# Result rows on every 16th partition, stored by one transfer

## The chip, the core and the metric

The kernel runs on one core of one Trainium2 chip. The metric is the device time of one execution in microseconds; lower is better. The time of the kernel before is the median of three runs. One more execution was recorded by the hardware profiler, and every row below comes from that one.

A core has a matrix engine (TensorE, PE in the profile), three engines for elementwise work (VectorE or DVE, ScalarE or ACT, GpSimd or POOL), and SyncE (SP), which here only issues transfers. Each engine runs its own list of instructions in order. Transfers between the main memory (HBM) and the on-chip memory (SBUF, 128 partitions) are issued by an engine and carried out by 16 DMA engines. TensorE writes to PSUM, an accumulator memory of 128 partitions.

## What is computed

One decoding step for two batches: attention over a cache of 4096 positions with 32 heads of 128, an output projection, a small feed-forward network, and a sigmoid gate that mixes the two. Cut to what matters:

```python
# x: (2, 1, 512); k_cache, v_cache: (2, 32, 4096, 128); wq: (512, 4096); wo: (4096, 512)
g = sigmoid((x * gate_w).sum(-1, keepdims=True))
q = (x @ wq) as (2, 32, 1, 128)
p = softmax(q @ k_cache^T * 128 ** -0.5)
a = (p @ v_cache) as (2, 1, 4096) @ wo
b = relu(x @ w1) @ w2                  # w1: (512, 1376), w2: (1376, 512)
out = g * a + (1 - g) * b              # (2, 1, 512), bfloat16
```

The K and V caches are 64 MB each; with the weights, 145.43 MB are read. The output is two rows of 512 numbers, 2 KB.

## The kernel before

The program is a list of operations for each engine, written out in one order by Python; a name given as `signal` marks an operation, and `waits` names the marks that another operation needs. An engine signals by counting up one semaphore, so a wait is for a count: whoever waits for a late operation of an engine also waits for all earlier ones of it.

**Loading.** SyncE issues almost all transfers, in one queue: wq, then 16 units of K and 16 of V, 4 MB each, into three buffers `kv` (L262 to L267). A unit is issued when the unit three places earlier has been used up: K units by four transposes on VectorE (`k_turn`, L380), V units by 32 matmuls (`v_unit`, L442). Behind the third unit stands w1, which waits for the q projection (`pe_q`, L267). Behind all units come the last 96 rows of w2 in eleven small pieces (L269, of 14 rows down to 2), wo in two halves (L270, L271), and the other rows of w2 in three pieces, w2b, w2c, w2d (L273).

**Start.** GpSimd clears and builds constants (L214 to L241); the last is `ptm`, 4096 elements per partition, marked `c_ptm`. ScalarE loads x and the gate's weights. VectorE copies the transposed x into `xTw` (L288), multiplies it for the gate (L289), and TensorE projects q (L320). The q values are spread into `qbuf` (L345), and the scores of the first K unit can start (L396).

**Middle.** Each K unit is transposed on VectorE and multiplied on TensorE; after four units a softmax is taken (L406 to L422), GpSimd spreads the probabilities into `ptm` (L425), and V units are multiplied with them. At the ninth transposed piece the first layer of the feed-forward network runs (`ffn_h`), and VectorE writes its result, scaled by one minus the gate, into `hT` (`ffn_relu`, L367 and L370). `hT` is [128, 11, 2]: eleven chunks of the hidden layer, the two batches side by side.

**End.** `o_gather` collects the attention output of a batch and writes it into `oW`, [128, 32, 2], a column for each batch (L483). Then `project` and `ffn_f` add up the result in one PSUM region of 128 partitions and 128 columns. They use `fin_row`: for each chunk r four matmuls, one for each block c of 128 output columns, with the two columns of `oW` or `hT` as weights. Block c goes to column group c of TensorE, so it lands on partitions 32c and 32c+1: batch b of block c is on partition 32c + b. That is 32 x 4 matmuls with wo and 11 x 4 with w2. `store` copies the region into `out_sb` (L507). SyncE then stores batch 0 and ScalarE batch 1, each as four rows of 128 numbers (`out_row`, L274 to L277), both behind that copy, and SyncE waits until both have arrived (L278).

Of the kernel before, what the change touches and what calls it, by code (L numbers as in the profile page):

```python
# [3 lines left out]
dt = mybir.dt  # L4
# [82 lines left out]
def bass_gated_mix__gqa_block_cached__dense_activation_relu__decode_kernel(  # L87
# [18 lines left out]
    sb = nc.alloc_sbuf_tensor  # L106
# [14 lines left out]
    wreg = sb("wreg", [128, 16384], dt.bfloat16)  # L121
    w2 = sb("w2", [128, 11, 512], dt.bfloat16)
# [18 lines left out]
    s4 = sb("s4", [32, 4, 128], dt.bfloat16)  # L141
    X2 = sb("X2", [128, 2, 8, 128], dt.float32)
    O_sb = sb("O_sb", [32, 2, 128], dt.bfloat16)
    oW = sb("oW", [128, 32, 2], dt.bfloat16)
    hT = sb("hT", [128, 11, 2], dt.bfloat16)
    out_sb = sb("out_sb", [128, 128], dt.bfloat16)

    PSF = nc.alloc_psum_tensor("PS", [128, 4096], dt.float32)
# [4 lines left out]
    def psf(p0, p1, c0, n):  # L153
        return PSF[p0:p1, c0:c0 + n]
# [8 lines left out]
    H_C0 = MISC + 72  # L163
    L_C0 = MISC + 96
    O_C0 = MISC + 128
    R_C0 = MISC + 256
    FIN_C0 = 0
# [4 lines left out]
    sem = {n: nc.alloc_semaphore("sem_" + n) for n in names}  # L172
# [4 lines left out]
    def marker(name):  # L177
        m = mk.get(name)
        if m is None:
            m = _Marker()  # L180
            mk[name] = m
        return m
# [14 lines left out]
    def freed(what):  # L197
        kind, u = what
        return marker(f"kt_{4 * u + 3}") if kind == "k" else marker(f"pe_v_{u}")


    def pool(fn, waits=(), signal=None):
        P.add("pool", fn, waits=[marker(w) for w in waits], signal=marker(signal) if signal else None)

    def dve(fn, waits=(), signal=None, dwaits=()):
        P.add("dve", fn, waits=[marker(w) for w in waits], signal=marker(signal) if signal else None, dwaits=dwaits)

    def act(fn, waits=(), signal=None, dwaits=()):
        P.add("act", fn, waits=[marker(w) for w in waits], signal=marker(signal) if signal else None, dwaits=dwaits)

    def pe(fn, waits=(), signal=None, dwaits=()):
        P.add("pe", fn, waits=[marker(w) for w in waits], signal=marker(signal) if signal else None, dwaits=dwaits)
# [5 lines left out]
         waits=["c_i16z"], signal="c_i16")  # L218
# [5 lines left out]
                                   in_=mask3[:].rearrange("p (t f) h c -> p t f h c", t=4)[:, :, 0],  # L224
                                   pattern=[[-32, 4], [-4, 4], [-1, 4]],
                                   compare_op=ALU.not_equal, fill=1.0, base=0, channel_multiplier=1),
         waits=["c_m3z"], signal="c_m3")
# [4 lines left out]
         waits=["c_s1"], signal="c_s2")  # L232
    pool(lambda g: g.affine_select(out=sell[:, 16:32], in_=sell[:, 16:32], pattern=[[8, 4], [32, 4]],
                                   compare_op=ALU.is_ge, fill=0.0, base=7, channel_multiplier=-1),
         waits=["c_s2"], signal="c_sell")
# [3 lines left out]
         waits=["c_s4z"], signal="c_s4")  # L239
    pool(lambda g: g.memset(selx[:], 0.0), signal="c_selx")  # L240
    pool(lambda g: g.memset(ptm[:], 0.0), signal="c_ptm")  # L241


    wq_in = A_wq.rearrange("(p t) n -> p (t n)", t=4)
# [11 lines left out]
    def sp(fn, waits=(), dwaits=()):  # L256
        P.add("sp", fn, waits=waits, dwaits=dwaits)
# [4 lines left out]
    for n, what in enumerate(order):  # L262
        waits = [freed(order[n - NSLOT])] if n >= NSLOT else []
        sp(lambda e, what=what: e.dma_start(kv[:, slot_of(what), :], unit_in(what)).then_inc(sem_slot[slot_of(what)], 16),  # L264
           waits=waits)
# [5 lines left out]
    sp(lambda e: e.dma_start(wreg[:, 8192:16384], wo_in[:, 8192:16384]).then_inc(sem["wo1"], 16))  # L271
    for name, r0, r1 in (("w2b", 0, 4), ("w2c", 4, 8), ("w2d", 8, 10)):
        sp(lambda e, name=name, r0=r0, r1=r1: e.dma_start(w2[:, r0:r1, :], w2a_in[:, r0:r1, :]).then_inc(sem[name], 16))  # L273
    def out_row(e, b):  # L274
        return e.dma_start(out[b:b + 1].rearrange("b s (c n) -> (b s c) n", n=128), out_sb[b::32, :]).then_inc(sem["out"], 16)

    sp(lambda e: out_row(e, 0), waits=[marker("dve_out")])  # L277
    sp(lambda e: e.wait_ge(sem["out"], 32))  # L278


    def gate():
# [82 lines left out]

    def ffn_relu():
        for b in range(2):
            dve(lambda v, b=b: v.tensor_scalar(out=hT[:, 0:10, b], in0=PSF[:, H_C0 + b:H_C0 + 20:2], scalar1=0.0,  # L367
                                               scalar2=gm[:, b:b + 1], op0=ALU.max, op1=ALU.mult),
                waits=["pe_h", "dve_gm"])
            dve(lambda v, b=b: v.tensor_scalar(out=hT[0:96, 10, b:b + 1], in0=psf(0, 96, H_C0 + 20 + b, 1), scalar1=0.0,  # L370
                                               scalar2=gm[0:96, b:b + 1], op0=ALU.max, op1=ALU.mult),
                waits=["pe_h", "dve_gm"], signal=f"dve_h{b}")

# [47 lines left out]
    def sm_spread(g):  # L421
        dve(lambda v: v.transpose(out=ET_sb[:, :], in_=E_sb[:, :]),  # L422
            waits=[f"act_exp{g}"] + ([f"pool_pt{g - 1}_3"] if g else []), signal=f"dve_et{g}")
        for hq in range(4):
            pool(lambda e, g=g, hq=hq: e.tensor_copy(  # L425
                out=ptm[32 * hq:32 * hq + 32, g % 2, :, :, :, hq, :],
                in_=ET_sb[32 * hq:32 * hq + 32, :].rearrange("p (r u a c) -> p r u a c", r=16, u=4, a=2)),
                waits=[f"dve_et{g}", "c_ptm"] + ([f"pe_v_{4 * g - 5}"] if g >= 2 else []), signal=f"pool_pt{g}_{hq}")


    def v_unit(v):
# [38 lines left out]
    def o_gather(b):  # L470
        for u in range(8):
            pe(lambda e, u=u, b=b: e.matmul(psf(0, 32, O_C0, 128), lhsT=selx[:, 28 - 4 * u:60 - 4 * u], rhs=X2[:, b, u, :],  # L472
                                            start=(u == 0), stop=(u == 7)),
               waits=[f"dve_x{8 * b + u}_3"] + ([f"dve_rinv{b}", "dve_selx"] if u == 0 else []),
               signal=(f"pe_O{b}" if u == 7 else None))
        dve(lambda v, b=b: v.tensor_scalar(out=O_sb[:, b, :], in0=psf(0, 32, O_C0, 128), scalar1=rinv[:, b:b + 1],
                                           scalar2=gb[0:32, b:b + 1], op0=ALU.mult, op1=ALU.mult),
            waits=[f"pe_O{b}", f"dve_rinv{b}", "dve_g"], signal=f"dve_O{b}")
        for dq in range(4):
            pe(lambda e, dq=dq, b=b: e.matmul(psf(0, 128, R_C0 + 32 * b, 32), lhsT=s4[:, dq, :], rhs=O_sb[:, b, 32 * dq:32 * dq + 32],  # L480
                                              start=(dq == 0), stop=(dq == 3), tile_position=(0, 0)),
               waits=([f"dve_O{b}", "c_s4"] if dq == 0 else []), signal=(f"pe_R{b}" if dq == 3 else None))
        dve(lambda v, b=b: v.tensor_copy(out=oW[:, :, b], in_=psf(0, 128, R_C0 + 32 * b, 32)), waits=[f"pe_R{b}"], signal=f"dve_oW{b}")  # L483


    def fin_row(r, first, last, lhsT, rhs, dw, waits, signal):
        for c in range(4):
            pe(lambda e, c=c: e.matmul(psf(32 * c, 32 * c + 2, FIN_C0, 128), lhsT=lhsT, rhs=rhs[:, c * 128:(c + 1) * 128],  # L488
                                       start=first, stop=last, tile_position=(0, 32 * c), skip_group_check=True),
               dwaits=(dw if c == 0 else []), waits=(waits if c == 0 else []), signal=(signal if c == 3 else None))  # L490

    def project():
        dve(lambda v: v.memset(psf(0, 128, FIN_C0, 128), 0.0), waits=["act_exp2"], signal="dve_fin0")
        for r in range(32):
            dw = {0: [(sem["wo0"], 16)], 16: [(sem["wo1"], 16)]}.get(r, [])
            fin_row(r, r == 0, False, oW[:, r, :], wreg[:, r * 512:(r + 1) * 512], dw,
                    ["dve_oW0", "dve_oW1", "act_exp3", "dve_fin0"] if r == 0 else [], None)

    def ffn_f():
        for n, r in enumerate([10, *range(10)]):  # L500
            m = 96 if r == 10 else 128
            dw = {10: [(sem["w2a"], 16 * len(W2A))], 0: [(sem["w2b"], 16)], 4: [(sem["w2c"], 16)], 8: [(sem["w2d"], 16)]}.get(r, [])
            fin_row(r, False, r == 9, hT[0:m, r, :], w2[0:m, r, :], dw, ["dve_h0", "dve_h1"] if n == 0 else [],
                    "pe_fin" if r == 9 else None)

    def store():
        dve(lambda v: v.tensor_copy(out=out_sb[:, :], in_=psf(0, 128, FIN_C0, 128)), waits=["pe_fin"], signal="dve_out")  # L507
        act(lambda e: out_row(e, 1), waits=["dve_out"])


    gate()
# [7 lines left out]
    for i in range(64):  # L519
        k_turn(i)  # L520
        if i >= 1:
            k_scores(i - 1)
        flush()
        if i == 8:
            ffn_h()
            late.append(ffn_relu)
        if i % 16 == 0 and i:
            g = i // 16 - 1
            sm_max(g)
            sm_exp(g)  # L530
            late.append(lambda g=g: sm_spread(g))
        if i == 40:
            o_denominator(0)
        if i >= 19 and i % 4 == 3:
            v = i // 4 - 4
            if i == 63:
                k_scores(63)
                sm_max(3)
                sm_exp(3)
                sm_spread(3)  # L540
            v_unit(v)
            late.append(lambda v=v: v_extract(v))
        if i == 52:
            late.append(lambda: o_gather(0))
# [41 lines left out]
```

## Time and profile before

| | |
|---|---|
| median of three runs | 347.62 us (347.56 to 348.02) |
| the profiled execution | 347.98 us |
| its span, first to last instruction | 346.5 us |
| busy in the span | PE 203.3 us, weight loads 76.7, DVE 182.4, ACT 13.9, POOL 20.9 |
| mean granted TensorE clock | 0.80 of full speed |
| read from HBM | 145.43 MB, 420 GB/s over the span |
| DMA queues, packets | q1 (SyncE's) 5816, q10 (ScalarE's) 14, instruction queues 12 |

Views used below: the page's slices (the span in 40 equal parts, each digit a busy share in tenths); the chain of waits, which follows the work that ended last back from the end, at each step to what released it; the timeline, which lists instructions in order of time (start, length, engine, line, operation, output<-inputs, shape, count, and in brackets the idle time before it and what ended it); waits by engine; and the DMA view of a short window, cut into 40 slices. "SPq" and "ACTq" are the queues from which SyncE and ScalarE issue transfers; the length of such a row is that of the issue, not of the transfer.

### The profile page before, as it was taken

To read this page: it belongs to the slowest core of one execution; us is meant where nothing else is said; L and a number is where in the kernel's file an instruction comes from. 1 tells how busy PE (TensorE), PEld (TensorE's weight loads), DVE (VectorE), ACT (ScalarE), POOL (GpSimd) and SP (SyncE) were. 2 spreads that over 40 slices of the span, in tenths; PEclk is the share of its full clock that TensorE was granted. 3 is DMA by queue.
4 is the path that set the end of the run, shared out by engine and by line. 5 is a ranking of instruction groups with operands and counts; after the bars stand their busy time and mean duration, and the time that the engine had idled before them with its cause. 6 is when DMAs were issued, how large, how long until landed. Compare 5 with 4: busy or idle time off the path is not lost.

```text
span 346.5 us, 3037 instructions
## 1 busy us (share of the span) xinstructions
PE 203.3 (59%) x1334; PEld 76.7 (22%) x1334; DVE 182.4 (53%) x177; ACT 13.9 (4%) x48; POOL 20.9 (6%) x36
## 2 busy tenths in 40 slices
PE   0419959773755729175855839074785839422283
PEld 0203333221211203021221313021421213110052
DVE  0848877990917356391918355391648367211120
ACT  1030000000000000000000000000000000000000
POOL 8400000020000000020000000020000000200000
PEclk9967978999685958789695969789696969666576
DMA  8999999999999999999999999999999999999993
GB/s 322 446 431 431 404 453 443 427 429 424 424 426 436 443 431 431 429 424 431 435 429 439 431 435 424 422 431 435 439 426 443 427 424 431 423 435 435 395 412 154
DMA packets 5842, 145.61 MB, mean 420 GB/s; under 512 B 739, under 2 KB 838, under 8 KB 1222
## 3 DMA queue, kind: packets, MB, share of 16 engines
q1 hardware_dynamic: 5816, 145.43, 98.1%
q8 instruction: 10, 0.16, 0.2%
q14 instruction: 2, 0.02, 0.0%
q10 hardware_dynamic: 14, 0.00, 0.0%
HBM read 145.43 MB, written 0.00 MB: 420 GB/s over the span
## 4 chain that ended last, share of the span: by engine, by line
DMA 70%; DVE 14%; PE 12%; SPq 2%; issue 1%; DVEq 0%
DMA kv<-in_A_k_cache_dram 53%; DVE kt L380 11%; DMA w<-in_B_w_dram 10%; PE PS L396 8%; DMA kv<-in_A_v_cache_dram 8%; PE PS L442 4%; SPq L269 1%; DVE X L456 1%; DVE mpad L406 1%; DVE ET L422 1%; PE PS L488 0%; SPq L264 0%; DVE X L453 0%; DVE mrow L408 0%; DVE mmax L409 0%
## 5 line engine op out<-in xcount | busy, mean ns | idle before, releaser
L396 PE MATMUL PS<-kt,qbuf 128*128 128x512 bf16 x512 | 149.8, 446 | 93.9 <-DVE kt L380 93.7
L380 DVE STREAM_TRANSPOSE kt<-kv 128x2048 f32<-128x2048 f32 x64 | 144.0, 2285 | 102.8 <-DMA kv<-in_A_k_cache_dram 102.2
L396 PEld LDWEIGHTS PS<-kt,qbuf 128*128 128x128 bf16 x512 | 50.5, 108 | 190.3 <-DVE kt L380 117.8
L442 PE MATMUL PS<-kv,ptm 128*16 128x512 bf16 x512 | 37.2, 442 | 23.0 <-DMA kv<-in_A_v_cache_dram 23.0
L425 POOL COPY ptm<-ET 32x512 bf16<-32x512 bf16 x16 | 9.7, 607 | 276.5 <-DVE ET L422 275.8
L442 PEld LDWEIGHTS PS<-kv,ptm 128*16 128x16 bf16 x512 | 12.8, 98 | 45.8 <-issue 35.7
L453 DVE TENSOR_SCALAR X<-PS,maskc 128x128 f32<-128x128 f32 x16 | 5.1, 319 | 30.9 <-PE PS L442 30.9
L456 DVE SCALAR_TENSOR_TENSOR X<-PS,maskc,X 128x128 f32<-128x128 f32 x48 | 16.8, 351 | 1.7
L351 ACT ACTIVATE qbuf<-PS 32x4 bf16<-32x4 bf16 x32 | 5.7, 178 | 110.7 <-PE PS L396 110.1
L417 ACT ACTIVATE E<-PS,negm 128x512 bf16<-128x512 f32 x4 | 2.7, 687 | 154.5 <-DVE negm L413 154.5
L472 PE MATMUL PS<-X,selx 128*32 128x128 f32 x32 | 5.3, 336 | 0.0
L283 PE MATMUL PS<-ident,x_sb 3*128 3x3 bf16 x4 | 0.3, 168 | 8.1 <-DMA x_sb<-in_gate_w_dram 8.1
L361 PE MATMUL PS<-xT,wreg 128*128 128x2 bf16 (+1 forms) x44 | 2.8, 200 | 3.6 <-DMA wreg<-in_B_w_dram 3.6
L472 PEld LDWEIGHTS PS<-X,selx 128*32 128x32 f32 x32 | 4.4, 142 | 1.9 <-issue 1.4
L286 DVE COPY xT<-PS 128x12 bf16<-128x12 bf16 x1 | 0.2, 169 | 8.4 <-PE PS L283 8.4
L488 PE MATMUL PS<-wreg,oW 128*2 128x128 bf16 x128 | 2.6, 242 | 3.4 <-DMA wreg<-in_A_wo_dram 3.0
L220 POOL MEMSET qbuf<- 128x5120 bf16 x1 | 4.4, 4370 | 0.0
L507 DVE CAST out_sb<-PS 128x128 bf16<-128x128 f32 x1 | 0.3, 291 | 7.6 <-PE PS L488 7.6
L288 DVE COPY xTw<-xT 128x8 bf16<-128x8 bf16 x1 | 3.9, 3862 | 0.0
L406 DVE TENSOR_REDUCE mpad<-PS 128x1 f32<-128x512 f32 x4 | 2.7, 676 | 2.1 <-PE PS L396 2.1
L361 PEld LDWEIGHTS PS<-xT,wreg 128*128 128x128 bf16 (+1 forms) x44 | 2.7, 161 | 4.1 <-DMA wreg<-in_B_w_dram 4.1
L289 DVE TENSOR_TENSOR xg<-xT 128x8 f32<-128x8 bf16 x1 | 3.6, 3629 | 0.0
(58 smaller groups left out, 40.5 us busy)
## 6 DMA issues: line engine op xcount, KB each, us to landing
kv<-in_A_k_cache_dram SPq DMA_DIRECT2D x16, 4096.0 KB, 26.2
kv<-in_A_v_cache_dram SPq DMA_DIRECT2D x16, 4096.0 KB, 18.7
wreg<-in_A_wq_dram SPq DMA_DIRECT2D x1, 4096.0 KB, 12.4
wreg<-in_A_wo_dram SPq DMA_DIRECT2D x2, 2048.0 KB, 29.9
wreg<-in_B_w_dram SPq DMA_DIRECT2D x1, 1376.0 KB, 27.3
w<-in_B_w_dram SPq DMA_DIRECT2D x2, 512.0 KB, 33.4
w<-in_B_w_dram SPq DMA_DIRECT2D x1, 256.0 KB, 33.9
x_sb<-in_A_x_dram ACTq DMA_DIRECT2D x1, 2.0 KB
```

Source lines behind the costliest of these rows:

```text
L220: pool(lambda g: g.memset(qbuf[:], 0.0), signal="c_qbuf")
L288: dve(lambda v: v.tensor_copy(out=xTw[:, :, 0:2], in_=xT), waits=["dve_xT", "c_xTw"], signal="dve_xTw")
L351: act(lambda a, out=out, src=src: a.activation(out=out, in_=src, func=ACT.Copy), waits=[f"pe_sc_{4 * uh + 3}"], signal=f"q_1_{uh}_{hq}")
L361: return e.matmul(psf(0, m, H_C0 + 2 * ft, 2), lhsT=cols, rhs=xT3[:, t, 0:2], start=(t == 0), stop=(t == 3))
L380: dve(lambda v: v.transpose(out=dst, in_=pairs[:, :, 32 * k:32 * k + 32, :]), waits=([f"pe_sc_{i - NKT}"] if i >= NKT else []), dwaits=([s ...
L396: pe(lambda e, j=j, pos=pos, c=c, cc=cc: e.matmul(psf(0, 128, (g % 2) * BANK, 512), lhsT=qbuf[:, u % 8, j, 32 - pos:160 - pos], rhs=kt16[: ...
L406: dve(lambda v, g=g: v.tensor_reduce(out=mpad[:, 0:1], in_=psf(0, 128, (g % 2) * BANK, 512), axis=AX.X, op=ALU.max), waits=[f"pe_sc_{16 * ...
L425: pool(lambda e, g=g, hq=hq: e.tensor_copy(out=ptm[32 * hq:32 * hq + 32, g % 2, :, :, :, hq, :], in_=ET_sb[32 * hq:32 * hq + 32, :].rearra ...
L442: pe(lambda e, n=n, t=t, a=a, r16=r16, grp=grp, u4=u4, rows=rows: e.matmul(psf(32 * t, 32 * t + 16, V_B * BANK, 512), lhsT=ptm[:, grp % 2, ...
L453: dve(lambda e, src=src, dst=dst: e.tensor_scalar(out=dst, in0=src, scalar1=maskc[:, 0:1], scalar2=None, op0=ALU.mult), waits=[f"pe_v_{v}" ...
L456: dve(lambda e, src=src, dst=dst, c=c: e.scalar_tensor_tensor(out=dst, in0=src, scalar=maskc[:, c:c + 1], in1=dst, op0=ALU.mult, op1=ALU.add),
L472: pe(lambda e, u=u, b=b: e.matmul(psf(0, 32, O_C0, 128), lhsT=selx[:, 28 - 4 * u:60 - 4 * u], rhs=X2[:, b, u, :], start=(u == 0), stop=(u ...
```

## The change

The two columns of weights move apart. `oW` and `hT` get 32 columns for each chunk instead of 2; batch 0 stands in column 0 and batch 1 in column 16. GpSimd clears both tensors once, behind `ptm`. The matmuls of `fin_row` take 17 columns as weights (0 to 16), so block c of batch b lands on partition 32c + 16b, and the 15 columns between give zeros. The result rows are then every 16th partition of `out_sb`, eight rows, and one transfer from SyncE stores them. ScalarE's transfer and `out_row` are gone; SyncE waits for one transfer. Operations that write `hT` and `oW` wait for the memsets, and the copies into `ptm` name the mark of the last memset, `c_oW`, in place of `c_ptm`. The order of all other instructions stays.

```diff
-    oW = sb("oW", [128, 32, 2], dt.bfloat16)
-    hT = sb("hT", [128, 11, 2], dt.bfloat16)
+    oW = sb("oW", [128, 32, 32], dt.bfloat16)
+    hT = sb("hT", [128, 11, 32], dt.bfloat16)
...
     pool(lambda g: g.memset(ptm[:], 0.0), signal="c_ptm")
+    pool(lambda g: g.memset(hT[:], 0.0), signal="c_hT")
+    pool(lambda g: g.memset(oW[:], 0.0), signal="c_oW")
...
-    def out_row(e, b):
-        return e.dma_start(out[b:b + 1].rearrange("b s (c n) -> (b s c) n", n=128), out_sb[b::32, :]).then_inc(sem["out"], 16)
-
-    sp(lambda e: out_row(e, 0), waits=[marker("dve_out")])
-    sp(lambda e: e.wait_ge(sem["out"], 32))
+    sp(lambda e: e.dma_start(out.rearrange("b s (c n) -> c (b s) n", n=128),
+                             out_sb[0::16, :]).then_inc(sem["out"], 16),
+       waits=[marker("dve_out")])
+    sp(lambda e: e.wait_ge(sem["out"], 16))
...
-            dve(lambda v, b=b: v.tensor_scalar(out=hT[:, 0:10, b], in0=PSF[:, H_C0 + b:H_C0 + 20:2], scalar1=0.0,
+            dve(lambda v, b=b: v.tensor_scalar(out=hT[:, 0:10, 16 * b], in0=PSF[:, H_C0 + b:H_C0 + 20:2], scalar1=0.0,
                                                scalar2=gm[:, b:b + 1], op0=ALU.max, op1=ALU.mult),
-                waits=["pe_h", "dve_gm"])
-            dve(lambda v, b=b: v.tensor_scalar(out=hT[0:96, 10, b:b + 1], in0=psf(0, 96, H_C0 + 20 + b, 1), scalar1=0.0,
+                waits=["pe_h", "dve_gm", "c_hT"])
+            dve(lambda v, b=b: v.tensor_scalar(out=hT[0:96, 10, 16 * b:16 * b + 1], in0=psf(0, 96, H_C0 + 20 + b, 1), scalar1=0.0,
...
-                waits=[f"dve_et{g}", "c_ptm"] + ([f"pe_v_{4 * g - 5}"] if g >= 2 else []), signal=f"pool_pt{g}_{hq}")
+                waits=[f"dve_et{g}", "c_oW"] + ([f"pe_v_{4 * g - 5}"] if g >= 2 else []), signal=f"pool_pt{g}_{hq}")
...
-        dve(lambda v, b=b: v.tensor_copy(out=oW[:, :, b], in_=psf(0, 128, R_C0 + 32 * b, 32)), waits=[f"pe_R{b}"], signal=f"dve_oW{b}")
+        dve(lambda v, b=b: v.tensor_copy(out=oW[:, :, 16 * b], in_=psf(0, 128, R_C0 + 32 * b, 32)), waits=[f"pe_R{b}", "c_oW"], signal=f"dve_oW{b}")
...
-            pe(lambda e, c=c: e.matmul(psf(32 * c, 32 * c + 2, FIN_C0, 128), lhsT=lhsT, rhs=rhs[:, c * 128:(c + 1) * 128],
+            pe(lambda e, c=c: e.matmul(psf(32 * c, 32 * c + 17, FIN_C0, 128), lhsT=lhsT, rhs=rhs[:, c * 128:(c + 1) * 128],
...
-            fin_row(r, r == 0, False, oW[:, r, :], wreg[:, r * 512:(r + 1) * 512], dw,
+            fin_row(r, r == 0, False, oW[:, r, 0:17], wreg[:, r * 512:(r + 1) * 512], dw,
...
-            fin_row(r, False, r == 9, hT[0:m, r, :], w2[0:m, r, :], dw, ["dve_h0", "dve_h1"] if n == 0 else [],
+            fin_row(r, False, r == 9, hT[0:m, r, 0:17], w2[0:m, r, :], dw, ["dve_h0", "dve_h1"] if n == 0 else [],
...
         dve(lambda v: v.tensor_copy(out=out_sb[:, :], in_=psf(0, 128, FIN_C0, 128)), waits=["pe_fin"], signal="dve_out")
-        act(lambda e: out_row(e, 1), waits=["dve_out"])
```

## The prediction

> **What bounds the kernel now.** I read the page's first line and its slices first, then the chain of waits in order of time, then the last microseconds instruction by instruction, and last the movement of the DMA engines in those microseconds.
>
> ```profile
> span 346.5 us, 3037 instructions
> ...
> DMA  8999999999999999999999999999999999999993
> ```
>
> The digits are the busy share of the 16 DMA engines in 40 slices: 9 from the second slice to the last but one. 145.43 MB must be read, and the kernel is the time that these reads take, plus a head and a tail. The change touches neither the reads nor their order, so only two places can matter: whatever could let the DMA queue run dry, and the tail after the last byte has come in. The tail in the chain of waits (start, length, what was waited for):
>
> ```profile
> 309.26 33.75 DMA w<-in_B_w_dram
> 343.01 0.04 issue
> 343.05 0.60 PE PS L488 x12
> 343.65 0.04 issue
> 343.69 0.41 PE PS L488 x8
> 344.10 0.02 issue
> 344.13 0.29 DVE out_sb L507
> ```
>
> The last weights (w2) end a wait at 343.05 and another at 343.69; after that come eight matmuls, one copy out of PSUM, and the two stores. The timeline of the stores (start, length, engine) and the wait list of SyncE's queue (total, times, longest):
>
> ```profile
> 344.44 0.60 SPq L275 DMA_DIRECT2D out_dram<-out_sb  x1
> 344.45 0.61 ACTq L275 DMA_DIRECT2D out_dram<-out_sb  x1
> ```
>
> ```profile
> SPq L278 <- DMA out_dram<-out_sb: 1.4, 1, 1.4
> ```
>
> So 0.41 + 0.29 + 0.60 + 1.4 = 2.7 us, with the gaps 2.8 us (343.69 to 346.5), is all that the output side of the change can work on. What the DMA engines did in it, from 345.5 to 346.3 in 40 slices of 0.02 us:
>
> ```profile
> GB/s 0 0 0 0 0 0 0 0 13 26 0 13 0 0 0 0 0 0 0 0 0 0 0 0 0 0 13 26 0 13 0 0 0 0 0 0 0 0 0 0
> ```
>
> Two equal bursts: slices 8 to 11 (345.66 to 345.74) and 26 to 29 (346.02 to 346.10). The view of each half says that the first is queue q1 (SyncE) and the second q10 (ScalarE), eight packets each. So although both issues run side by side, the second row leaves 18 slices, 0.36 us, after the first, and the kernel waits for it.
>
> **The change, part by part.**
>
> *ScalarE's store goes (gain).* The second burst falls away: -0.36 us. Nothing is queued behind it on ScalarE, whose last other work ended at 295.2 us.
>
> *SyncE's store carries eight rows instead of four.* Issues of like size with nothing beside them are the small w2 pieces of L269; the chain shows that of 8 rows and that of 4 rows (the seventh and the tenth piece):
>
> ```profile
> 306.27 0.29 SPq L269
> 307.28 0.29 SPq L269
> ```
>
> Eight rows cost no more to issue than four. Four rows made eight packets inside 0.08 us; queue q10 carried 14 packets in the whole run, which is rows plus one end packet for each row for x (2+2), the gate (1+1) and the output (4+4), so each row had an engine of its own. With two rows on each of four engines there are 12 packets. A row's packet starts and ends within about a slice, so I add +0.02 us; bounds 0 and +0.08 (a second burst's full length).
>
> *The issue itself.* It took 0.60 us beside the other and 0.29 us for a lone piece. If the first burst was held back by the sharing, it now starts up to 0.31 us sooner; if the issues were served one after the other, SyncE's first, it starts when it did. The bursts stand 0.36 us apart, close to one lone issue after the other and far from being interleaved, so I take 0; ends 0 and -0.31 us. The Trainium skill, "DMA: Bandwidth & Descriptors", section Issuing engines are not separate DMA queues, says that issuing from several engines saves only the sequencers' time for issuing, and since that is usually small, by this rule dropping the second queue would gain nothing and the sum would be about +0.06 us; the bursts say otherwise here.
>
> *Weights of 17 columns.* All 172 loads of L488 change from 2 to 17 columns. The nearest rows are the 16-column loads of the V products, also four column groups and at the same granted clock of 0.50:
>
> ```profile
> 319.25 0.14 PEld L442 LDWEIGHTS PS<-kv,ptm 128*16 128x16 bf16 x8 [7.01 <-issue]
> 343.69 0.10 PEld L488 LDWEIGHTS PS<-w,hT 128*2 128x2 bf16 x8 [0.33 <-DMA w<-in_B_w_dram]
> ```
>
> Eight loads take 0.14 instead of 0.10 us: +0.04 us on the path, for the last eight matmuls. The 128 projection loads and the first 20 of the feed-forward end before 343.05 with PE idle for 0.46 us; 5 ns each on the 84 after 340.5 is 0.42 us, just covered. Of the 16 at 343.05, PE has 0.04 us to spare before 343.69; were none of their loads hidden, they add 0.08. Bounds 0 and +0.12 us. 17 rows of output cost nothing more: 32 matmuls of 512 columns into 16 rows take 3.59 us, 0.45 for four, 0.11 for each 128 columns, and the 16 of 128 columns into 2 rows at 343.05 take 0.60 us, 0.15 for four: fewer rows are no faster. The skill's "TensorE: Matmul & The Clock Gate", section LDWEIGHTS (loading the stationary operand), gives a load as columns divided by 1.2 ns, an estimate of 12.5 ns more for each, 0.10 us for eight, which would make the whole sum -0.24 us.
>
> *Strided copies.* L483 writes oW every 64 bytes instead of every 4; it takes 0.20 us at 336.09, and the projection it feeds waits for weights until 340.56, 3 us later. L367 and L370 at 50.12 cost four times 0.2 us, with 32 elements at most: nothing. Without those waits a slower L483 would be paid in full.
>
> *Two more memsets on GpSimd.* 352 and 1024 elements behind ptm's 4096 at 3.50 us (0.85 ns each): 0.3 + 0.9 = 1.2 us, ending near 13.7 instead of 12.46. The new waits on them stand before L367 (50.12), L483 and the first L425 (73.40): over 36 us late, none stops anything queued behind. But they hold something else:
>
> ```profile
> 8.63 3.86 DVE L288 COPY xTw<-xT 128x8 bf16<-128x8 bf16 x1
> 8.86 3.63 DVE L289 TENSOR_TENSOR xg<-xT 128x8 f32<-128x8 bf16 x1
> 8.96 3.50 POOL L241 MEMSET ptm<- 128x4096 bf16 x1
> ...
> 19.93 1.27 ACT L345 ACTIVATE qbuf<-PS 32x32 bf16<-32x32 bf16 x4 [0.49 <-PE PS L339]
> ```
>
> ```profile
> 25.32 11.76 PE L396 MATMUL PS<-kt,qbuf 128*128 128x512 bf16 x40 [5.43 <-DVE kt L380]
> ```
>
> A copy and a product of eight elements took 3.6 to 3.9 us and ended at 12.49, with ptm's memset. They will now probably end near 13.7, and q with them: 21.20 + 1.2 = 22.4 us. The first scores start at 25.32 behind the first K transpose, so 4.1 us of cover eats 1.2. The w1 load, issued behind q at 19.92, moves to 21.1, in a queue that has K units to bring until 44.0, when VectorE's wait for the third one ends. Cost 0; gone the cover, 1.2 us.
>
> Sum: -0.36 + 0.02 + 0 + 0.04 + 0 = **-0.30 us**. The profiled execution took 347.98 us (span 346.5 and 1.5 around it) and would take 347.7; it lies 0.36 above the median, so I put the sum on the median: 347.62 - 0.30 = **347.3 us**.
>
> **The rivals.**
>
> A, the lone issue also sends sooner. For: 0.29 against 0.60 us, and x's first packets at the head came 0.9 us after its issue began, SyncE's row 1.2 us after. Against: x's issue was shared too. Sum -0.36 - 0.31 + 0.06 = -0.61: 347.0 us.
>
> B, nothing is gained: the later burst was only the slower write, and eight rows in one transfer take as long as two of four (+0.36 given back). For: eight rows must leave either way. Against: a burst is 0.08 us long, so the 0.36 is not the writing. 347.62 + 0.06 = 347.7 us.
>
> C, slower: GpSimd's longer memset run. The DVE copies wait for its end, q is late, the scores are late, K slots come free late and the DMA queue runs dry once. Price 1.2 us, less the output's 0.3: 348.5 us; laid bare, with nothing saved at the end, 348.8. It decides only when q slips by more than 4.1 us and then by more than the 12 us for which K units are still queued when the fourth K unit is issued (31.87 to 44.0). Nothing in the profile brings 1.2 near that.
>
> That the store does not change as said is excluded for the issue: a single output transfer remains. Whether its eight rows spread over four engines is open; on one engine, eight rows and an end at about 0.02 us make 0.2 us, which lies between the likeliest case and B.
>
> **How the numbers follow.** Likeliest case 0.43, A 0.28, B 0.18, C 0.10, anything larger on the gaining side 0.01. Less than 0.2%, about 0.7 us, is what a measurement of this kernel can tell from no change: 346.92 and 348.32 are the edges. The likeliest and B lie inside. A stands 0.1 us from the edge, and the three runs before already differ by 0.46 us, so about half of A counts as faster, 0.14, and with the larger gains and the likeliest's lower tail 0.18. Slower is C, 0.10. The same: 0.72. The likeliest's own range is its bounds -0.67 to -0.16 (0 to +0.08 and 0 to +0.12 at their upper ends): 346.95 to 347.5. With A's scatter below and B's above (348.02 was seen before) I widen to **346.8 to 348.0**; C is left out.
>
> **What would show it.** One burst at the end with q1 alone in it, 12 packets, and q10 at 6 packets in all; the span's end 2.5 us (A: 2.2) behind the start of the last eight matmuls instead of 2.8. SyncE's output issue near 0.29 us: A is right if its burst also starts under 1.0 us after the issue. Eight 17-column loads in about 0.14 us. The copy into xTw and the product behind it ending near 13.7 us while the first scores stay at 25.3 and the last w2 wait at 343.7. The forecast is wrong if the first scores move, if a slice of the DMA row falls, or if the one transfer takes over 2 us from issue to the end as the two did.

## The result and the profile after

| | before | changed |
|---|---|---|
| median | 347.72 us (347.51 to 348.06, 20 runs) | 347.19 us (346.84 to 347.82, 20 runs) |
| the profiled execution | 347.98 us, span 346.5 | 347.82 us, span 346.6 |

The ratio is 0.9985, with a 95% interval of 0.9978 to 0.9992: 0.15% faster, 0.53 us between the medians. That is less than the 0.2% that the prediction gave as the least that can be told from no change, but the interval leaves out 1. The forecast was 347.3 us, in a range of 346.8 to 348.0; the change itself was forecast as -0.30 us.

The profiled execution of the changed kernel is the slowest of its 20: its last weights came in 0.38 us later than in that of before. So the tails can be compared, but not the two spans. The page of the changed kernel, queue lines (packets, MB, share):

```profile
q1 hardware_dynamic: 5820, 145.43, 98.1%
q8 instruction: 10, 0.16, 0.2%
q14 instruction: 2, 0.02, 0.0%
q10 hardware_dynamic: 6, 0.00, 0.0%
```

ScalarE's queue q10 has 6 packets where it had 14, SyncE's q1 four more: the eight rows went out as 12 packets, eight rows and four ends, which fits four DMA engines with two rows each. The timeline of its last microseconds:

```profile
343.43 1.03 PE L489 MATMUL PS<-w,hT 128*17 128x128 bf16 x24 [0.20 <-DMA w<-in_B_w_dram]
344.07 0.12 PEld L489 LDWEIGHTS PS<-w,hT 128*17 128x17 bf16 x8 [0.31 <-DMA w<-in_B_w_dram]
344.52 0.29 DVE L508 CAST out_sb<-PS 128x128 bf16<-128x128 f32 x1 [7.92 <-PE PS L489]
344.84 0.65 SPq L276 DMA_DIRECT2D out_dram<-out_sb  x1
```

And the DMA engines from 346.0 to 346.4, in 40 slices of 0.01 us:

```profile
GB/s 0 0 0 0 0 0 0 0 0 0 0 26 26 26 26 26 26 26 0 26 0 0 0 0 0 0 0 0 0 0 0 0 0 0 0 0 0 0 0 0
```

One burst, 346.11 to 346.20; the second is gone. From the last w2 wait (344.07) to the span's end (346.57) it is 2.50 us, against 2.79 before. Piece by piece, before and changed, the packets to the width of a slice (0.02 and 0.01 us):

| | before | changed |
|---|---|---|
| last eight matmuls, to the start of the copy | 0.44 | 0.45 |
| copy, to the start of the issue | 0.31 | 0.32 |
| issue's start to the first packet | 1.22 | 1.27 |
| first packet to the last | 0.44 | 0.09 |
| last packet to the end of the span | 0.37 | 0.38 |

So the tail gives 0.29 us, close to the 0.30 that was forecast. The medians differ by 0.53. Where the other quarter of a microsecond comes from can't be seen inside the span. But each run of the changed kernel comes with its own span, and the difference, the time around the span, answers: it was 1.25 us (1.20 to 1.39) in these 20 runs, and 1.5 us in the profiled run of before, the only one of before's here that has a span. The experiments follow this up, with the span and the time around it told apart.

### The profile page after: what moved, and what is told of

Its sections match the earlier page's. It is cut to its first block, busy times and chain, and to the rows that moved or that the text cites. A ratio compares the mean times of both kernels' runs of the same rounds, so it can differ in the third digit from the quotient of the medians.

```text
span 346.6 us, 3023 instructions
## 1 busy us (share of the span) xinstructions
PE 201.8 (58%) x1318; PEld 77.5 (22%) x1334; DVE 183.6 (53%) x177; ACT 13.9 (4%) x48; POOL 22.1 (6%) x38
## 4 chain that ended last, share of the span: by engine, by line
DMA 71%; DVE 16%; PE 10%; SPq 2%; issue 1%; DVEq 0%
DMA kv<-in_A_k_cache_dram 53%; DVE kt L381 12%; DMA w<-in_B_w_dram 10%; DMA kv<-in_A_v_cache_dram 8%; PE PS L397 6%; PE PS L443 4%; DVE X L457 1%; SPq L271 1%; DVE mpad L407 1%; DVE ET L423 1%; PE PS L489 0%; DVE X L454 0%; SPq L266 0%; DVE mrow L409 0%; DVE mmax L410 0%
## 5 line engine op out<-in xcount | busy, mean ns | idle before, releaser
L397 PE MATMUL PS<-kt,qbuf 128*128 128x512 bf16 x496 | 146.6, 447 | 95.1 <-DVE kt L381 92.2
L289 DVE COPY xTw<-xT 128x8 bf16<-128x8 bf16 x1 | 5.1, 5054 | 0.0
L489 PE MATMUL PS<-wreg,oW 128*17 128x128 bf16 x128 | 2.8, 257 | 3.8 <-DMA wreg<-in_A_wo_dram 3.2
L290 DVE TENSOR_TENSOR xg<-xT 128x8 f32<-128x8 bf16 x1 | 4.9, 4858 | 0.0
```

What stands on the lines that cost most here:

```text
L289: dve(lambda v: v.tensor_copy(out=xTw[:, :, 0:2], in_=xT), waits=["dve_xT", "c_xTw"], signal="dve_xTw")
L290: dve(lambda v: v.tensor_tensor(out=xg[:], in0=xT, in1=xT3[:, :, 2:3].to_broadcast([128, 4, 2]), op=ALU.mult), waits=["dve_xT"], signal="d ...
L397: pe(lambda e, j=j, pos=pos, c=c, cc=cc: e.matmul(psf(0, 128, (g % 2) * BANK, 512), lhsT=qbuf[:, u % 8, j, 32 - pos:160 - pos], rhs=kt16[: ...
```

## The experiments

Each kernel but one was timed beside the kernel before, on the same chip. The table gives means over the runs, with standard errors; "list" is the length of ScalarE's list of instructions against the changed kernel's. The first row holds the runs of before that stood beside e1 to e12; those beside the changed kernel have no spans.

| kernel | runs | list | span, us | around it, us | total, us | ratio, 95% interval |
|---|---|---|---|---|---|---|
| before (beside these) | 102 | +1 | 346.22 ± 0.02 | 1.51 ± 0.01 | 347.73 | |
| changed | 20 | 0 | 345.98 ± 0.05 | 1.25 ± 0.01 | 347.23 | 0.9985 [0.9978, 0.9992] |
| e1, two queues again | 11 | +1 | 346.25 ± 0.05 | 1.51 ± 0.01 | 347.76 | 0.9999 [0.9990, 1.0008] |
| e2, the start alone | 11 | +1 | 346.31 ± 0.05 | 1.51 ± 0.01 | 347.82 | 1.0001 [0.9992, 1.0009] |
| e3, two on SyncE | 11 | 0 | 346.52 ± 0.05 | 1.27 ± 0.02 | 347.79 | 1.0000 [0.9991, 1.0009] |
| e4, one on ScalarE | 11 | +1 | 346.05 ± 0.05 | 1.48 ± 0.01 | 347.53 | 0.9994 [0.9985, 1.0003] |
| e5, late ScalarE copy | 11 | +1 | 346.05 ± 0.04 | 1.49 ± 0.02 | 347.53 | 0.9994 [0.9985, 1.0003] |
| e6, ScalarE load midway | 11 | +1 | 345.99 ± 0.03 | 1.49 ± 0.02 | 347.48 | 0.9993 [0.9984, 1.0002] |
| e7, no ScalarE transfer | 11 | -2 | 346.10 ± 0.04 | 1.30 ± 0.02 | 347.39 | 0.9991 [0.9983, 1.0000] |
| e9, e4 with a load moved | 11 | 0 | 346.00 ± 0.03 | 1.27 ± 0.02 | 347.27 | 0.9987 [0.9978, 0.9996] |
| e10, before with it moved | 11 | 0 | 346.24 ± 0.05 | 1.27 ± 0.01 | 347.50 | 0.9993 [0.9984, 1.0002] |
| e11, early ScalarE copy | 11 | +1 | 345.98 ± 0.04 | 1.48 ± 0.01 | 347.46 | 0.9993 [0.9984, 1.0001] |
| e12, 32 copies to VectorE | 11 | -32 | 346.00 ± 0.03 | 1.28 ± 0.02 | 347.28 | 0.9990 [0.9981, 0.9999] |

The profiles bear the column "list" out: computing instructions and transfers of ScalarE together are 50 in the changed kernel, e3, e8, e9 and e10, 51 in before, e1, e2, e4, e5, e6 and e11, 48 in e7 and 18 in e12.

### e1: the store alone undone

```diff
-    sp(lambda e: e.dma_start(out.rearrange("b s (c n) -> c (b s) n", n=128),
-                             out_sb[0::16, :]).then_inc(sem["out"], 16),
-       waits=[marker("dve_out")])
-    sp(lambda e: e.wait_ge(sem["out"], 16))
+    def out_row(e, b):
+        return e.dma_start(out[b:b + 1].rearrange("b s (c n) -> (b s c) n", n=128), out_sb[16 * b::32, :]).then_inc(sem["out"], 16)
+    sp(lambda e: out_row(e, 0), waits=[marker("dve_out")])
+    sp(lambda e: e.wait_ge(sem["out"], 32))
...
+        act(lambda e: out_row(e, 1), waits=["dve_out"])
```

> The changed kernel with the store alone undone: rows still every 16th partition, 17 columns, memsets; batch 0 leaves from SyncE and batch 1 from ScalarE again. Theory S (the whole gain is the store): the gain is gone, ratio to before 1.000 to 1.0003; two packet bursts 0.36 us apart, 2.8 us from the last w2 wait to the span's end, and the time around the span back at the 1.5 us of before's profiled run instead of the 1.25 us of the changed kernel's runs. Theory H (part of the gain, about 0.23 us, comes from the start, where q is 1.2 us later): ratio about 0.9993, with 1.25 us around the span.

The DMA engines from 345.5 to 346.5 in this kernel, slices of 0.025 us:

```profile
GB/s 0 0 0 0 0 0 0 0 0 0 10 21 0 10 0 0 0 0 0 0 0 0 0 0 0 20 11 10 0 0 0 0 0 0 0 0 0 0 0 0
```

Two bursts, 15 slices or 0.37 us apart. Ratio 0.9999: with memsets, 17 columns and spread rows all in place, the gain is gone, in the span (346.25) and around it (1.51). The whole gain goes with this edit, and the 17 columns cost nothing that these runs can tell. The edit does two things, though: it splits the store, and it puts an instruction back on ScalarE's list. e3 to e12 part the two.

### e2: the longer memset run alone, in the kernel before

```diff
+    pool(lambda g: g.memset(pad1[:], 0.0), signal="c_pad1")   # 352 columns
+    pool(lambda g: g.memset(pad2[:], 0.0), signal="c_pad2")   # 1024 columns
...
-                waits=[f"dve_et{g}", "c_ptm"] ...
+                waits=[f"dve_et{g}", "c_pad2"] ...
```

> The kernel before with two more GpSimd memsets of 352 and 1024 elements behind ptm, on tensors that nothing reads; nothing else. Theory S: the two copies on VectorE end near 13.7 us, q is 1.2 us later, first scores at 25.2 to 25.3 us all the same, ratio 1.000. Theory H: ratio 0.9993. The slower rival of the prediction (the delay reaches the DMA queue): up to 1.2 us, ratio 1.0034.

Its timeline at the start:

```profile
8.65 5.08 DVE L292 COPY xTw<-xT 128x8 bf16<-128x8 bf16 x1
8.87 4.86 DVE L293 TENSOR_TENSOR xg<-xT 128x8 f32<-128x8 bf16 x1
8.97 3.50 POOL L243 MEMSET ptm<- 128x4096 bf16 x1
12.43 0.38 POOL L244 MEMSET pad<- 128x352 bf16 x1
12.76 0.94 POOL L245 MEMSET pad<- 128x1024 bf16 x1
...
25.12 1.46 PE L400 MATMUL PS<-kt,qbuf 128*128 128x512 bf16 x3 [3.99 <-DVE kt L384]
```

The two small VectorE operations end with the last memset, at 13.73, 1.24 us later than before. The first scores start at 25.12 behind the K transpose, as ever, and the ratio is 1.0001. The delay is real and costs nothing; the slower rival falls, and so does theory H.

### e3: two transfers, both from SyncE

`out_row` is that of e1.

```diff
-    sp(lambda e: e.dma_start(out.rearrange(...), out_sb[0::16, :]).then_inc(sem["out"], 16), waits=[marker("dve_out")])
-    sp(lambda e: e.wait_ge(sem["out"], 16))
...
+    sp(lambda e: out_row(e, 0), waits=[marker("dve_out")])
+    sp(lambda e: out_row(e, 1))
+    sp(lambda e: e.wait_ge(sem["out"], 32))
```

> The changed kernel with the store as two transfers of four rows, both issued by SyncE, one behind the other. Theory S as predicted (a transfer behind another leaves about one issue later): two bursts, the second 0.3 to 0.65 us behind the first (an issue took 0.29 for small loads and 0.65 for the lone store), span 0.3 to 0.6 us longer than the changed kernel's. The time around the span tells what it depends on: 1.25 us if on ScalarE having an issue at the end, 1.5 us if on there being two transfers.

The DMA engines from 345.0 to 346.4 in this kernel, slices of 0.035 us:

```profile
GB/s 0 0 0 0 0 0 0 0 0 0 0 15 15 0 0 0 0 0 0 0 0 0 0 0 0 0 0 15 15 0 0 0 0 0 0 0 0 0 0 0
```

The second burst stands 16 slices, 0.56 us, behind the first; the issues took 0.60 and 0.50 us. In one queue the second row leaves about one issue later; in two queues it left 0.36 us later. The span is 0.54 us longer than the changed kernel's (346.52 to 345.98), and 0.27 us longer than with two queues (e1, 346.25): the second queue as such had been a help, and the gain comes from there being one transfer. Around the span it is 1.27 us: two transfers as such don't cost the quarter.

### e4: the one transfer from ScalarE

```diff
-    sp(lambda e: e.dma_start(out.rearrange(...), out_sb[0::16, :]).then_inc(sem["out"], 16), waits=[marker("dve_out")])
     sp(lambda e: e.wait_ge(sem["out"], 16))
...
+        act(lambda e: e.dma_start(out.rearrange(...), out_sb[0::16, :]).then_inc(sem["out"], 16), waits=["dve_out"])
```

> The changed kernel with its one transfer issued by ScalarE instead of SyncE; SyncE only waits for it. One burst, span as in the changed kernel (2.5 us from the last w2 wait). If the time around the span depends on ScalarE having an issue at the end: 1.5 us, ratio about 0.9992; if on the number of transfers: 1.25 us, ratio about 0.9985 as the changed kernel.

The DMA engines from 345.0 to 346.0, slices of 0.025 us:

```profile
GB/s 0 0 0 0 0 0 0 0 0 0 0 0 31 21 21 10 0 0 0 0 0 0 0 0 0 0 0 0 0 0 0 0 0 0 0 0 0 0 0 0
```

One burst. Span 346.05, like the changed kernel's within the errors; around it 1.48. So the two parts of the gain come apart: one transfer instead of two shortens the span, and something about ScalarE the time around it.

### e5 and e6: is it late work, or a transfer?

```diff
+    scr = sb("scr", [128, 128], dt.bfloat16)
...
+        act(lambda a: a.activation(out=scr[:, 0:32], in_=out_sb[:, 0:32], func=ACT.Copy), waits=["dve_out"])
```

> The changed kernel with one small ScalarE copy (128x32) behind out_sb, into a tile that nothing reads; no transfer from ScalarE. Theory L (ScalarE being at work late costs 0.25 us around the span): 1.5 us around the span, total 347.45 to 347.5, as with the store on ScalarE. Theory Q (a late transfer of ScalarE's queue costs it): 1.25 us, total as the changed kernel, 347.2, span unchanged at 346.0.

```diff
...
+    sp(lambda e: e.wait_ge(sem["mid"], 16))
...
+            act(lambda e: e.dma_start(scr[0:4, :], A_x[0:1].rearrange("b s (c n) -> (b s c) n", n=128)).then_inc(sem["mid"], 16))
```

> The changed kernel with a load of four small rows issued by ScalarE in the middle of the run (at the 41st K transpose), into a tile that nothing reads; SyncE waits for it at the end, when it has long arrived. Theory Q in its wide form (any further transfer of ScalarE's queue costs 0.25 us around the span): 1.5 us. Theory L, or Q only for a transfer at the very end: 1.25 us, total 347.2.

Both give 1.49 us around the span. e5 has late work and no transfer, e6 a transfer and no late work. Theory L explains the first and not the second, theory Q the second and not the first. What they share is one more instruction in ScalarE's list. That became theory N.

### e7: no transfer from ScalarE at all

```diff
-    act(lambda e: e.dma_start(x_sb[0:2, :], ...).then_inc(sem["x"], 16))
-    act(lambda e: e.dma_start(x_sb[2:3, :], ...).then_inc(sem["gw"], 16))
     sp(lambda e: e.dma_start(wreg[:, :], wq_in).then_inc(sem["wq"], 16))
+    sp(lambda e: e.dma_start(x_sb[0:2, :], ...).then_inc(sem["x"], 16))
+    sp(lambda e: e.dma_start(x_sb[2:3, :], ...).then_inc(sem["gw"], 16))
```

> The changed kernel with the loads of x and the gate's weights moved from ScalarE to SyncE, behind wq, so that ScalarE issues no transfer at all. If the time around the span falls with each use of ScalarE's queue: under 1.25 us, perhaps 1.0. If only a late use counts: 1.25 us. Span: x arrives behind wq, near 11 us instead of 8; q has 2.5 to 4 us to spare, so the first scores stay near 25.2 and the span at 346.0.

1.30 us around the span: two instructions fewer win nothing more. x came near 13 us, later than expected, which q could bear.

### e8: what a small transfer's issue costs

Nine more transfers from SyncE stand behind the store, each issued once the one before has arrived; the last stores the result again. In order: the store again; eight rows of neighbouring partitions to the interleaved places of the result, then to places in a row; a load mirroring the store, twice; a store of two 1 KB rows; a load of four neighbouring rows; a store of every 32nd partition to places in a row (the form of before); the store again.

`good` stands for the interleaved places of the result; `form` issues a transfer and waits for it.

```diff
...
+    form(2, lambda e: e.dma_start(good, out_sb[0::16, :]))
+    form(3, lambda e: e.dma_start(good, out_sb[0:8, :]))
+    form(4, lambda e: e.dma_start(out.rearrange("b s (c n) -> (b s c) n", n=128), out_sb[0:8, :]))
...
+    form(9, lambda e: e.dma_start(out[0:1].rearrange("b s (c n) -> (b s c) n", n=128), out_sb[0::32, :]))
+    form(10, lambda e: e.dma_start(good, out_sb[0::16, :]))
```

> The changed kernel with nine more small transfers from SyncE behind the store, each issued after the one before has arrived, so its own time can't be compared: the same store again; eight rows from neighbouring partitions, to the same places and to places in a row; the mirrored load of eight rows twice; a store of two rows of 1 KB; a load of four rows; a store of four rows; the good store again. If the 0.65 us of the store's issue is a first touch: the second takes about 0.3. If it is a property of a store: all stores 0.5 to 0.65, loads 0.25 to 0.35. If it is the partition step: the neighbouring rows take less. From issue to SyncE's release: 1.7 us for a store (0.65 + 1.1).

The timeline (start, length of the issue); the distance to the next start is the whole transfer with SyncE's release:

```profile
344.24 0.66 SPq L277 DMA_DIRECT2D out_dram<-out_sb  x1
345.97 0.53 SPq L286 DMA_DIRECT2D out_dram<-out_sb  x1
347.58 0.65 SPq L287 DMA_DIRECT2D out_dram<-out_sb  x1
349.32 0.32 SPq L288 DMA_DIRECT2D out_dram<-out_sb  x1
350.56 0.59 SPq L289 DMA_DIRECT2D scr<-in_A_x_dram  x1
352.43 0.54 SPq L290 DMA_DIRECT2D scr<-in_A_x_dram  x1
354.17 0.26 SPq L291 DMA_DIRECT2D out_dram<-x_sb  x1
355.33 0.26 SPq L292 DMA_DIRECT2D scr<-in_A_x_dram  x1
356.71 0.57 SPq L293 DMA_DIRECT2D out_dram<-out_sb  x1
```

The first row is the kernel's own store. It isn't a first touch (0.53 the second time), nor a matter of store or load (0.54 and 0.59 for the mirrored load). Issues took 0.26 to 0.32 us where rows follow each other on both sides (the fourth, seventh and eighth row), and 0.53 to 0.66 where partitions are stepped or the rows are interleaved in HBM, either of which is enough (the ninth and the third row). For eight rows the whole transfer took 1.24 us in the plain form and 1.74 in the form with interleaved places, from the same partitions. Each form stands in one execution here; only the form of before is seen again by itself, in e3, where SyncE issued two such stores one behind the other in 0.60 and 0.50 us.

### e9, e10, e11: the length of ScalarE's list

e9 is e4, and e10 the kernel before, each with the gate's load moved from ScalarE to SyncE; e11 is the changed kernel with a ScalarE copy more near 15 us.

```diff
-    act(lambda e: e.dma_start(x_sb[2:3, :], gate_w.rearrange("(o d) -> o d", o=1)).then_inc(sem["gw"], 16))
     sp(lambda e: e.dma_start(wreg[:, :], wq_in).then_inc(sem["wq"], 16))
+    sp(lambda e: e.dma_start(x_sb[2:3, :], gate_w.rearrange("(o d) -> o d", o=1)).then_inc(sem["gw"], 16))
```

> The kernel with one store from ScalarE (1.48 us around the span) and the load of the gate's weights moved from ScalarE to SyncE, behind wq: ScalarE's list is as long as in the changed kernel, and still ends with a store. Theory N (a list of ScalarE's that is longer than the changed kernel's by one or more costs 0.25 us around the span, whatever the instruction is and wherever it stands): 1.25 us around the span, total 347.2 to 347.3, ratio 0.9985 to 0.9988. If a store or other late work on ScalarE costs it by itself: 1.48 us as without the move, ratio 0.9994.

> The kernel before with nothing but that one load moved from ScalarE to SyncE, behind wq; two stores as before. Theory N: 1.25 us around the span, span as before (346.2), ratio 0.9993. Otherwise: 1.5 us, ratio 1.000.

```diff
...
+        act(lambda a: a.activation(out=scr[:, 0:32], in_=ident16[:, 0:32], func=ACT.Copy), waits=["c_i16"])
```

> The changed kernel with one small ScalarE copy more in the first 20 us, into a tile that nothing reads; store as changed. Theory N: 1.5 us around the span though nothing at the end differs, span 346.0, ratio 0.9993. If only what ScalarE does from the middle on counts: 1.25 us, ratio 0.9985.

All three fall as theory N says. e9 stores from ScalarE, and is at 1.27 around the span. e10 is the kernel before in all that the change is about, with both stores and a span of 346.24, and is at 1.27. e11 has the changed kernel's end, and is at 1.48.

### e12: does the step repeat?

```diff
-            act(lambda a, out=out, src=src: a.activation(out=out, in_=src, func=ACT.Copy),
+            dve(lambda v, out=out, src=src: v.tensor_copy(out=out, in_=src),
                 waits=[f"pe_sc_{4 * uh + 3}"], signal=f"q_1_{uh}_{hq}")
...
-        if k == 3 and u < 8:
-            q_second(u)
...
+        if i % 4 == 2 and 6 <= i <= 34:
+            q_second((i - 6) // 4)
```

> The changed kernel with the 32 small copies of batch 1's q (L352) moved from ScalarE to VectorE, each set of four three K turns later than before, where its scores have long been read: ScalarE's list is 32 instructions shorter. If the step of 0.25 us repeats with the length of the list: 1.0 us or less around the span, total 346.9 to 347.0, faster than both kernels. If the changed kernel's length is below the only step that matters: 1.25 us, total 347.2. VectorE has room (busy 53%), so the span should stay at 346.0; were the copies in the way of the K transposes, it grows.

1.28 us around the span: 32 instructions fewer win nothing more, so in the lengths tried there is one step, between the changed kernel's list and one instruction more. Longer lists than that were not tried. The span is unharmed. No kernel tried beats the changed one.

## Why the prediction was right, and what it missed

*The bound.* Reads fill the DMA queue, and only the tail could change: right for the span; what lies around the span was not thought of (below). The span fell by 0.24 us (346.22 to 345.98), and in the table it moves with the form of the store only.

*The second burst, -0.36 us: right.* It is gone in the changed kernel's window, comes back in e1, and moves to 0.56 us behind the first when both rows go through one queue (e3). In the two profiled tails the stretch from first to last packet went from 0.44 to 0.09 us. Why the second row left just 0.36 us later stays open: the prediction found it close to one lone issue, 0.29 us, but an issue of this form by itself took 0.50 to 0.60 (e3, e8).

*Two rows on each of four engines, +0.02: right,* with 12 packets inside 0.09 us against eight inside 0.08.

*The issue, 0: 0.05 us too low, and wrong in its row.* The prediction set the lone w2 pieces at 0.29 us against 0.60 in company and kept a gain of up to 0.31 as a bound and as rival A. The store alone took 0.65 us, and its burst started 1.27 us after the issue instead of 1.22, so later and not earlier. e8 shows why the row was a bad one: those pieces have neighbouring partitions and rows in order, the output of the changed kernel has neither. Company was not what made 0.60 of it, for the same form by itself took 0.57 (e8) and 0.60 (e3); the layout was.

*The 17 columns, +0.04: right, a little high.* Eight loads took 0.12 us instead of 0.10, and the stretch to the copy 0.45 instead of 0.44. The lengths of these eight loads by themselves (shortest, median and longest in ns), before and changed:

```profile
L488 PEld LDWEIGHTS PS<-w,hT x8: 79/79/79, 343.7 to 343.7; 128*2 128x2 bf16 x8
L489 PEld LDWEIGHTS PS<-w,hT x8: 91/94/98, 344.1 to 344.1; 128*17 128x17 bf16 x8
```

A load became 12 to 19 ns longer, so the rule for one load that the prediction took from the Trainium skill ("TensorE: Matmul & The Clock Gate", section LDWEIGHTS (loading the stationary operand)), 12.5 ns more by its estimate, is not far off here. Taking it eight times was the mistake: the eight loads overlap, and together they took 0.02 us more and not 0.10.

For the 84 matmuls ahead of the w2 waits the prediction added 5 ns each, 0.42 us, just covered. They were busy for 2.28 us instead of 2.03 and left TensorE 0.20 us idle instead of 0.46, but that is no price of the columns: the granted clock was 0.55 there (340.9 to 343.43), against 0.61 before (340.5 to 343.05). At equal clocks the 64 projection matmuls took 1.06 us with 2 columns and 1.07 with 17 (before at 336.53, changed at 336.65, clock 1.00), and at a clock of 0.50, in e10 with 2 columns and in e6 with 17:

```profile
340.23 1.88 PE L488 MATMUL PS<-wreg,oW 128*2 128x128 bf16 x64 [2.86 <-DMA wreg<-in_A_wo_dram]
340.25 1.89 PE L491 MATMUL PS<-wreg,oW 128*17 128x128 bf16 x64 [3.00 <-DMA wreg<-in_A_wo_dram]
```

So 0.01 us for 64 matmuls was measured, where 5 ns each would be 0.32 us.

*The strided copies, 0: right,* though L483 is now 0.30 us long instead of 0.20; the projection behind it waited 3.2 us for its weights.

*The memsets, 0: right.* 12.46 became 13.7 and q came 1.4 us later (22.64), 0.2 more than said. The first scores of the changed kernel stayed where they were, behind the K transpose:

```profile
25.22 1.03 PE L397 MATMUL PS<-kt,qbuf 128*128 128x512 bf16 x2 [3.89 <-DVE kt L381]
```

e2 shows that alone it costs nothing. The last w2 wait, said to stay at 343.7, ended at 344.07 here; in the profiles of the other kernels with memsets of this length it ended anywhere from 343.26 (e4) to 343.78 (e1), so a single profile can't tell a shift of it from scatter.

*What was missed: the time around the span.* "It lies 0.36 above the median, so I put the sum on the median" takes the 1.5 us around the span as fixed. It fell by a quarter of a microsecond, 1.51 to 1.25, as much as the store gave. e4 to e12 show that it depends on the length of ScalarE's list: every kernel with one instruction more than the changed one has 1.48 to 1.51, every one with as many or fewer 1.25 to 1.30, wherever the instruction stands and whatever it does. The lists of the other engines don't explain it: GpSimd's two more memsets leave it at 1.51 (e2), one or two more transfers on SyncE at 1.27 to 1.30 (e3, e7), one fewer at 1.48 (e4). The change took one instruction from ScalarE's list by moving a store; e10 gets the same quarter without touching the store. That this one instruction lies at the step was luck. Two terms of a like size, -0.29 in the tail, which was foreseen, and about -0.25 around the span, which was not, make the 0.53 us between the medians; the means of the table give -0.24 and -0.26. What happens in that time stays open: no view used here reaches outside the span.

*Luck in the number.* The forecast of 347.3 us lies 0.1 us from the measured 347.19, though a term of 0.25 us was missing. Part of that is the base: the median of before's three runs was 347.62, that of its 20 runs 347.72. From the second base the same sum gives 347.4. The change itself, -0.30 us against -0.53, is the fairer measure.

*The rivals.* A falls by the start of the burst, 1.27 us after the issue where A needed under 1.0. B falls by the first-to-last packets, 0.09 us where B needed as long as before. C falls by e2.

## What to carry to other kernels

Where a kernel ends with small stores, look at the packets of its last microsecond and not at the lengths of the issues: two stores issued side by side left 0.36 us apart here, and in one queue 0.56, and one transfer for all rows won most of the 0.36. Before differences of a few tenths are put down to a mechanism, split each run into its span and the time around it; a list shorter by one instruction gave as much here as the single store itself. And price an issue by one whose rows lie alike on both sides, not by one of like size.

## What the runs showed of the hardware that was not expected

- A step of about 0.2 to 0.25 us in the time outside the span, between two lengths of ScalarE's list that differ by one instruction (1.25 to 1.30 us in seven kernels, with e8's single run at 1.26 among them; 1.48 to 1.51 in seven others, before among them); 32 instructions fewer brought no second step.
- An issue of 0.26 to 0.32 us for small transfers whose rows follow each other on both sides, 0.50 to 0.66 us for those stepped over partitions or interleaved in HBM, for loads and stores alike (e3, e8).
- After the last packet of the store that the slices show, the span went on for 0.37 to 0.38 us, in which SyncE only waited for its release.
- A weight load of 17 columns took 91 to 98 ns where one of 2 took 79, but eight of them together only 0.12 us instead of 0.10, at a granted clock of 0.50.
